# Two halves for the third query unit's channel mixing and for one GELU group (two-layer attention and mixer kernel)

## The chip, the core and the metric

The kernel runs on one core of a Trainium2 chip. The metric is the device time of one execution in microseconds. Five engines run their own instruction streams and meet at semaphores: TensorE (PE) multiplies, ScalarE (ACT) evaluates functions such as exp, tanh and GELU, VectorE (DVE) does elementwise work and moves results out of PSUM, GpSimd (POOL) computes here the powers for the normalisations, and SyncE (SP) issues the DMAs.

## The reference

Two layers; each is an attention block and a mixer with an MLP, both with residuals, over 2048 positions of 448 channels. The attention has 16 heads of 28 channels. Both layers use the same weights.

```python
# A: attention on the normalised x          (wo, wqkv)
p = softmax(einsum("bhqd,bhkd->bhqk", q, k) * 28**-0.5)
x = x + einsum("bhqk,bhkd->bhqd", p, v) @ wo
# B: mixer and MLP on y = layernorm(x)      (w1, w2, w3, w4)
h  = gelu(layernorm(y) @ w1)
hs = concat(four channel groups of h, shifted by -1, +1, -2, +2 positions) @ w2
x1 = y + hs
x  = x + x1 + gelu(layernorm(x1) @ w3) @ w4
```

## The kernel before

**Tiles and units.** A tile is 128 positions; there are 16. Attention works on query units: four units of four tiles, the last of layer 1 halved in two units of two tiles. Units are counted from 0, so the third is unit 2 with the tiles 8 to 11. For each unit and each group of four heads PE makes scores for one key tile after the other (L1243), ACT takes their exponential (L1269, two or three score blocks of 512 columns in one instruction), and PE multiplies with the values (L1318). Fifty score blocks get their exponential on DVE (L1159 to L1172). The sums over keys are normalised on DVE, and the output projection (L1386 and on) adds to the residual x_res.

**The mixer behind a unit.** When a unit's attention is done, `t_outproj` calls `spawn_mixer`, which starts two kinds of task. `t_mixA` normalises a list of tiles, transposes them, multiplies with w1 and applies the GELU; within the stretch this GELU is made of DVE operations around one tanh on ACT (`tanh_gelu`, L1406 to L1437). The transposes are a DMA on SP for more than two tiles, and PE transposes (L872, copied out at L877) for one or two (`n <= 2`). `t_mixB` takes groups of tiles from the table `MIXB`: it waits for mixA of the tiles beside them (the shift by positions), makes x1 (`t_x1`, w2), transposes, multiplies with w3 in 14 groups whose results DVE moves to h2T (L1609), and after a GELU on ACT multiplies with w4 (14 matmuls a tile). In layer 1 its transposes are on PE too for one or two tiles.

**The GELU groups.** An entry of `MIXB` is (tiles, first column slot in h2T, group). `t_gelu` waits until w3 is done for all entries of a group and then issues one GELU for each entry, back to back, so that exp's and GELU's tables are exchanged once per group. Entries without a group (the last three tiles) take their GELU straight from PSUM.

**Who sets the order.** A planner in the file (`Sched`) builds the instruction stream of every engine at build time from task generators with assumed durations, and tracks all reads and writes to place the semaphores. It plans some rounds; each uses latest starts from the round before, and `MOVES` lists, for two of them, times and random seeds at which the due times of some tasks are shifted. Other seeds give another order of the same work. Where the planner sees PE idle too long it inserts fill matmuls that compute nothing needed (L1686). In the setup some operations may run on ACT or on DVE (`alt`), as the planner finds it.

**The head.** Before the first exponential the kernel loads x and wqkv, casts wq and wk into padded form (L741, L743), normalises and transposes the first four tiles, and projects keys, queries and values of the first chunk (L662, L665 with wk_pad, wq_pad, wv). **The tail** after the last exponential is the last units' output projection, mixer and MLP, and the output stores.

Of the kernel before, what the change touches and what calls it, by code (L numbers as in the profile page):

```python
# [496 lines left out]
def build_kernel(nc, A_x, A_wqkv, A_wo, B_x, B_w1, B_w2, B_w3, B_w4, out, n_layers=2):  # L497
# [11 lines left out]
    BIAS2 = 127.0  # L509
    WSH = 60.0 / LN2 + BIAS2  # L510
    DEFER = 4
    OFFL = ((48, 104, 6), (104, 300, 6), (372, 411, 6), (480, 520, 6), (520, 600, 8), (640, 731, 6))
    EXPA = (0.07826797 * 128) ** (1 / 3)
    EXPB = EXPA * 0.30457565 / 0.07826797
# [3 lines left out]
    ROUNDS = 2  # L518
    MOVES = [
        [  # L520
            (0.00, 453789), (32.56, 797911), (48.62, 659924), (64.69, 318104), (161.61, 114807), (210.38, 918064), (274.54, 530462), (290.66, 355311),
            (306.74, 234581), (323.12, 940320), (355.32, 335807), (374.64, 262209), (390.75, 238473), (423.02, 904553), (455.14, 951219), (503.31, 353319),
            (519.32, 830975), (551.41, 87786), (567.44, 416536), (583.44, 953034), (599.45, 216641), (615.49, 123806), (647.71, 418804), (663.92, 737035),
            (679.96, 651820), (728.32, 723986), (760.36, 640052), (792.53, 320335), (808.54, 626538), (840.72, 608440), (876.72, 136641), (908.79, 748207),
            (924.80, 42066), (941.01, 696523), (957.18, 398650), (973.27, 754326), (989.39, 285914), (1006.15, 600949), (1022.18, 988087),
        ],
        [
            (0.00, 951844), (12.28, 444188), (24.31, 919282), (48.56, 963253), (60.73, 133731), (72.83, 242907), (84.87, 106861), (108.92, 980702),
            (133.43, 460163), (145.58, 489327), (157.59, 422286), (181.65, 400901), (205.74, 788872), (217.97, 738730), (230.17, 462143), (254.24, 124206),
            (266.43, 963194), (278.52, 170914), (290.57, 109033), (302.68, 722504), (314.77, 35337), (327.20, 201463), (339.27, 676445), (351.28, 477925),  # L530
            (366.34, 151894), (390.42, 723936), (402.46, 162311), (414.47, 812461), (426.52, 379211), (438.52, 122860), (450.61, 425742), (462.66, 818907),
            (475.22, 535633), (487.27, 1519), (499.30, 306556), (516.33, 162929), (540.73, 587464), (552.75, 370357), (564.75, 1541), (576.96, 165268),
            (589.01, 579738), (601.02, 905581), (613.58, 714602), (625.65, 696422), (637.83, 751260), (649.91, 220258), (661.93, 654573), (698.68, 121787),
            (710.99, 422722), (723.01, 142611), (735.05, 984297), (759.08, 14052), (771.10, 359944), (783.26, 84680), (795.40, 873617), (807.52, 132498),
            (819.69, 932845), (843.77, 139438), (855.88, 608162), (893.87, 524650), (905.88, 743153), (918.47, 135596), (942.74, 639761), (954.85, 280336),
            (966.90, 914942), (978.92, 414440), (1015.44, 282794), (1027.57, 425880), (1039.68, 28012),
        ],
    ]
    GATE1 = ('qr', 0)
# [12 lines left out]
    HALVED = [(4 * c, 4) for c in range(NCH - 1)] + [(NT - 4, 2), (NT - 2, 2)]  # L552
    MIXB = [
        [([0, 1, 2], 0, 0), ([3, 4, 5, 6], 3, 0), ([7, 8, 9, 10], 0, 1), ([11, 12], 4, 2), ([13, 14, 15], 0, 2)],
        [([0, 1, 2], 4, 0), ([3, 4, 5, 6], 0, 0), ([7, 8, 9, 10], 3, 1), ([11, 12], 0, 2), ([13], 2, None), ([14, 15], 3, None)],
    ]
    WHOLE = [(4 * c, 4) for c in range(NCH)]
    UNITS = [WHOLE] * (n_layers - 1) + [HALVED]
# [15 lines left out]
    def c_b2b(n):  # L574
        return 0.07 + n * 0.00026
# [8 lines left out]
    with st:  # L584
# [72 lines left out]
        def op(eng, dur, fn, reads=(), writes=(), **kw):  # L657
            return (eng, dur, fn, list(reads), list(writes), kw)
# [165 lines left out]
        def ln_stats(t):  # L824
            yield op("dve", 0.55, lambda e: e.bn_stats(out=st6[:, t, :], in_=x_res[:, t, :]), reads=[("x", t)], writes=[("st6", t)])  # L825
            yield op("dve", 0.2, lambda e: e.bn_aggr(out=mv[:, t, :], in_=st6[:, t, :]), reads=[("st6", t)], writes=[("mv", t)])
# [305 lines left out]
        def on_dve(n):  # L1132
            if len(grans[n]) < 3:
                return False
            L, u, g, p, kts, first, last = segs[grans[n][2][0]]
            return 1 <= grans[n][2][1] <= len(kts) * UNITS[L][u][1] // 4 - 4 and any(a <= n < b and n % m == 0 for (a, b, m) in OFFL)

# [142 lines left out]
        def t_pv(si):  # L1280
# [6 lines left out]
            for i in range(len(kts)):  # L1287
                if i % grp == 0:
                    now = [h for h in held if h[0] + DEFER <= i * nt // 4]
                    held = [h for h in held if h not in now]  # L1290
# [161 lines left out]
        def t_mixA(L, tiles, direct):  # L1452
            n = len(tiles)
            NW = 128 * n
            t0 = tiles[0]
            for t in tiles:
                for tp in (t - HR - 1, t - HR, t - HR + 1):
                    if 0 <= tp < NT:
                        yield ("wait", ("x1", L, tp))
                    elif L > 0 and 0 <= tp + NT < NT and NT % HR == 0:  # L1460
                        yield ("wait", ("x1", L - 1, tp + NT))
            for t in tiles:
                yield ("wait", ("x1r", L, t))
                yield from ln_stats(t)
            xs = yield from acq_xn(n, direct)
            sl = slice(t0, t0 + n)
            mk = [("mst", t) for t in tiles]
            mvk = [("mv", t) for t in tiles]
            yield op("dve", 0.1, lambda e: e.tensor_scalar(out=mst[:, sl, T1], in0=mv[:, sl, 1], scalar1=1.0 + EPS, scalar2=EPS * EPS, op0=ALU.mult, op1=ALU.add), reads=mvk, writes=mk)
            yield op("pool", 0.42 + 0.15 * n, lambda e: e.tensor_tensor(out=mst[:, sl, R12], in0=mst[:, sl, T1], in1=neghalf[:, 0:n], op=ALU.pow), reads=mk + [("neghalf",)], writes=mk)  # L1470
            yield ("spawn", t_r1(tiles), 3, True)
            for i, t in enumerate(tiles):
                yield op("dve", 0.12 + c_b2b(D), lambda e, t=t, i=i: e.tensor_scalar(out=blk(xs.v[:, i, :]), in0=b112(x_res[:, t, :]), scalar1=mv[:, t, 0:1], scalar2=mst[:, t, R12:R12 + 1],
                                                                          op0=ALU.subtract, op1=ALU.mult),
                         reads=[("x", t), ("mv", t), ("mst", t)], writes=[(xs.key, i)])
            xt = yield from acq_xt(n, direct)
            yield from transposes(xs, xt, n, direct or n <= 2)
            yield ("rel", xs.res)
            c0 = 2 + 128 * (t0 % HR)
            def group(grp):  # L1480
                b = yield ("acq", MISC, [xt.key])
                for (fc, rows) in KCM:
                    yield mm(NW, 112, lambda a, z, b=b: ps[a:z, bi(b), 0:NW], lambda a, z, fc=fc, rows=rows: w1[0:rows, fc, 112 * grp + a:112 * grp + z],
                        xt.v[0:rows, 0:n, fc, :], fc == 0, fc == 3,
                        reads=[xt.key, ("w1",)], writes=[("ps", bi(b))], touch=[b])
                hk = hkeys(grp, t0, tiles[-1])
                if direct:
                    yield op("act", c_act(NW), lambda e, grp=grp, b=b: e.activation(out=hT[0:112, grp, c0:c0 + NW], in_=ps[0:112, bi(b), 0:NW], func=ACT.Gelu_apprx_tanh),
                             reads=[("ps", bi(b))], writes=hk, touch=[b], tab="gelu")
                else:  # L1490
                    yield from tanh_gelu(hT[0:112, grp, c0:c0 + NW], ps[0:112, bi(b), 0:NW], 112, NW, b, hk)
                    return
                yield ("rel", b)
            yield from par(3, [group(grp) for grp in range(4)])
            yield ("rel", xt.res)
            for t in tiles:
                yield ("sig", ("mixA", L, t))
                if t % HR == 0 and t > 0:
                    yield ("spawn", t_halo(L, t), 2)
# [154 lines left out]
        def spawn_mixer(L, u):  # L1654
            t0, n = UNITS[L][u]
            end = u == len(UNITS[L]) - 1
            ta = list(range(t0, t0 + n))
            if end and L == n_layers - 1:
                for t in ta:
                    yield ("spawn", t_mixA(L, [t], True), 3)  # L1660
            else:
                yield ("spawn", t_mixA(L, ta, False), 3)
            last = max(t0 + n - 2, 0) if not end else NT - 1
            for (tiles, h0, k) in MIXB[L]:
                if max(t0 - 1, 0) <= tiles[-1] <= last and (tiles[-1] < NT - 1 or end):
                    yield ("spawn", t_mixB(L, tiles, h0, k, 3), 3)
# [110 lines left out]
```

## Time and profile before

| | us |
|---|---|
| median of 4 runs (1068.8, 1062.56, 1070.72, 1069.67) | 1069.24 |
| the profiled execution | 1068.8 |
| its span from first to last instruction | 1067.1 |
| ACT busy | 1019.0 (95%) |
| PE busy, fill matmuls L1686 among it | 1029.4 (96%), 139.7 |
| DVE busy | 745.4 (70%) |
| POOL busy | 58.0 (5%) |
| GELU instructions L1650 (9) | 44.9 |
| DMA transposes issued on SP, L866 | 29 records, 3.7 to landing (median) |

The profile describes one execution. A group's line gives its source line, engine and operation, tiles out<-in with their shapes and the count; behind the bar the busy time, the mean duration in ns of one instruction, and the time that the engine sat idle just before such instructions with what ended the wait. Consecutive ACT instructions overlap by a little, so the mean duration of one is more than the distance from start to start. Lines of a timeline begin with the start and the length in us. In a table of windows each engine's busy time is followed by its instruction count, and the columns at the end are the granted TensorE clock (1.00 is full), the DMA share and GB/s.

### The profile page before, as it was taken

How to read it: one execution, taken by the hardware profiler on the slowest of the kernel's cores; microseconds unless marked ns; L12 is line 12 of the kernel's file. 1: busy time of each engine (PE TensorE's matmuls, PEld its weight loads, DVE VectorE, ACT ScalarE, POOL GpSimd, SP SyncE). 2: the span in 40 equal slices, each digit the busy share in tenths (PEclk: the TensorE clock that was granted, in tenths of full speed). 3: DMA queues.
4: the chain of work that ended last, by engine and by line, in shares of the span. 5: the costliest groups of instructions: out<-in, count | busy, mean ns of one | idle time of the engine just before them, and what ended most of it. 6: DMA issues, size and time to landing. Idle time of an engine off the chain costs nothing.

```text
span 1067.1 us, 21975 instructions
## 1 busy us (share of the span) xinstructions
PE 1029.4 (96%) x9469; PEld 396.9 (37%) x9485; DVE 745.4 (70%) x1683; ACT 1019.0 (95%) x940; POOL 58.0 (5%) x78
## 2 busy tenths in 40 slices
PE   8999999999999999999999999999999999999998
PEld 4333333333333333332333433333333333444455
DVE  6976468876887547887579666557978864677644
ACT  5999999999999999999989999999999999999983
POOL 1100000000000001010001000000000000010000
PEclk9999899999999999999989999999999999999999
DMA  4233140000001001100111101212020001110000
GB/s 115 61 110 100 35 121 20 2 16 21 21 2 21 1 3 39 35 22 1 20 41 31 26 11 60 70 43 48 21 46 1 21 1 33 30 22 2 2 19 23
DMA packets 70714, 35.09 MB, mean 33 GB/s; under 512 B 56472, under 2 KB 65048, under 8 KB 70616
## 3 DMA queue, kind: packets, MB, share of 16 engines
q1 hardware_dynamic: 70616, 33.68, 12.6%
q8 instruction: 74, 1.21, 0.5%
q14 instruction: 24, 0.20, 0.1%
HBM read 12.70 MB, written 7.08 MB: 19 GB/s over the span
## 4 chain that ended last, share of the span: by engine, by line
ACT 53%; PE 41%; DVE 4%; DMA 1%; issue 1%; SPq 0%; POOL 0%; POOLq 0%; DVEq 0%; ACTq 0%
ACT PT L1269 46%; PE ps L662 11%; PE ps L1243 11%; PE ps L1318 9%; PE ps L1686 6%; ACT h2T L1650 4%; PE ps L665 3%; ACT L1650 1%; ACT gt L1433 1%; DMA h2T<-in_A_wqkv_dram 1%; ACT L1269 1%; DVE hT L1406 0%; DVE sq L941 0%; DVE qT L970 0%; PE ps L872 0%
## 5 line engine op out<-in xcount | busy, mean ns | idle before, releaser
L1269 ACT ACTIVATE PT<-ps 128x1024 bf16<-128x1024 f32 (+1 forms) x821 | 918.4, 1228 | 13.2 <-PE ps L1243 8.9
L1243 PE MATMUL ps<-qT,kT 32*128 32x512 bf16 (+1 forms) x2304 | 323.3, 362 | 15.5 <-ACT PT L1269 11.3
L1318 PE MATMUL ps<-PT,vaug 128*32 128x512 bf16 (+1 forms) x2253 | 268.9, 364 | 3.6 <-ACT PT L1269 2.3
L1243 PEld LDWEIGHTS ps<-qT,kT 32*128 32x128 bf16 x2304 | 80.7, 91 | 263.9 <-ACT PT L1269 160.3
L1686 PE MATMUL ps<-ones_bf 128*128 128x256 bf16 x893 | 139.7, 279 | 2.9 <-DVE hot L696 1.1
L1318 PEld LDWEIGHTS ps<-PT,vaug 128*32 128x32 bf16 x2253 | 67.6, 94 | 135.7 <-issue 82.8
L662 PE MATMUL ps<-xT,w 112*128 112x512 bf16 (+6 forms) x574 | 115.6, 320 | 1.2 <-DVE h2T L1609 0.4
L1609 DVE CAST h2T<-ps 128x512 bf16<-128x512 f32 (+2 forms) x126 | 73.6, 584 | 58.7 <-PE ps L662 43.6
L1686 PEld LDWEIGHTS ps<-ones_bf 128*128 128x128 bf16 x893 | 73.6, 99 | 68.7 <-issue 50.6
L665 PE MATMUL ps<-xT,w 112*32 112x512 bf16 (+3 forms) x808 | 71.9, 350 | 0.3 <-DVE qT L970 0.2
L662 PEld LDWEIGHTS ps<-xT,w 112*128 112x128 bf16 (+1 forms) x574 | 46.1, 104 | 46.0 <-issue 24.3
L662 PE MATMUL ps<-w,h2T 128*128 128x448 bf16 x257 | 61.2, 354 | 0.4 <-ACT h2T L1606 0.4
L1159 DVE TENSOR_SCALAR t<-ps 128x512 int32<-128x512 f32 x50 | 34.3, 686 | 32.7 <-PE ps L1243 32.2
L665 PE MATMUL ps<-w,h2T 128*32 128x448 bf16 x764 | 49.4, 353 | 3.8 <-ACT h2T L1650 2.4
L1650 ACT ACTIVATE h2T<-h2T 128x7168 bf16<-128x7168 bf16 (+2 forms) x9 | 44.9, 5012 | 0.1
L1347 DVE SCALAR_TENSOR_TENSOR uin<-uin,fct,ps 128x512 f32<-128x512 f32 x20 | 14.8, 742 | 38.8 <-PE ps L1318 38.2
L1568 POOL TENSOR_TENSOR mst<-mst,neghalf 128x1 f32<-128x1 f32 x32 | 25.5, 803 | 296.9 <-DVE mst L1566 296.9
L825 DVE BATCH_NORM_STATS2 st<-x_res 128x6 f32<-128x448 bf16 x64 | 38.9, 613 | 1.6 <-DMA x_res<-in_A_x_dram 0.9
L1626 DVE TENSOR_TENSOR uin<-x_res,ps 128x448 bf16<-128x448 bf16 x16 | 9.8, 615 | 38.9 <-PE ps L662 20.9
L1167 DVE SCALAR_TENSOR_TENSOR gt<-gt 128x512 f16<-128x512 f16 x50 | 34.5, 691 | 1.3
L1172 DVE SCALAR_TENSOR_TENSOR PTD<-t,gt 128x512 uint16<-128x512 int32 x50 | 34.5, 689 | 1.3
L1168 DVE SCALAR_TENSOR_TENSOR gt<-gt 128x512 f16<-128x512 f16 x50 | 34.4, 688 | 1.3
(143 smaller groups left out, 1043.5 us busy)
## 6 DMA issues: line engine op xcount, KB each, us to landing
uin<-uscr SPq DMA_DIRECT2D x20, 256.0 KB, 2.7
uscr<-u_sb SPq DMA_DIRECT2D x12, 256.0 KB, 2.0
uscr<-uin SPq DMA_DIRECT2D x8, 256.0 KB, 2.1
out_dram<-uin SPq DMA_DIRECT2D x16, 112.0 KB, 1.7
w<-in_B_w_dram SPq DMA_DIRECT2D x4, 392.0 KB, 3.7
x_res<-in_A_x_dram SPq DMA_DIRECT2D x3, 448.0 KB, 8.6
w<-in_B_w_dram SPq DMA_DIRECT2D x2, 448.0 KB, 7.2
h2T<-in_A_wqkv_dram SPq DMA_DIRECT2D x2, 392.0 KB, 5.9
```

The source lines that it names most:

```text
L662: return e.matmul(out=dst(0, m), lhsT=lhs(0, m), rhs=rhs, start=start, stop=stop)
L665: return [e.matmul(out=dst(a, min(m, a + 32)), lhsT=lhs(a, min(m, a + 32)), rhs=rhs, start=start, stop=stop, tile_position=(0, a)) for a i ...
L825: yield op("dve", 0.55, lambda e: e.bn_stats(out=st6[:, t, :], in_=x_res[:, t, :]), reads=[("x", t)], writes=[("st6", t)])
L1167: yield op("dve", c_ps(512), lambda e: e.scalar_tensor_tensor(out=ex, in0=fx, scalar=-EXPA, in1=fx, op0=ALU.add, op1=ALU.mult), reads=[((" ...
L1168: yield op("dve", c_ps(512), lambda e: e.scalar_tensor_tensor(out=ex, in0=fx, scalar=EXPB, in1=ex, op0=ALU.add, op1=ALU.mult), reads=[(("g ...
L1172: yield op("dve", 0.06 + c_ps(512), lambda e: e.scalar_tensor_tensor(out=PTD[:, slot, :].bitcast(mybir.dt.uint16), in0=t32[:, :], scalar=2 ...
L1243: yield op("pe", 0.005 if ph == h else 0.012 + W / 2400.0, lambda e, bk=bk, r0=32 * j, g=g, kc=kc, q0=q0, W=W, c0=W * h: e.matmul(out=ps[: ...
L1269: yield op("act", e_dur(n), lambda e, b0=b0, p0=p0, cnt=cnt: e.activation(out=PT[:, p0:p0 + cnt, :], in_=ps[:, b0:b0 + cnt, :], func=ACT.E ...
L1318: yield op("pe", nt * 0.054 if item in late else 0.004 + nt * 0.0133, lambda e, j=j, rhs=rhs, vs=vs, i=i: e.matmul(out=ps[32 * j:32 * j + ...
L1609: yield op("dve", c_ps(NW), lambda e, fch=fch, b=b: e.tensor_copy(out=h2T[:, fch, hoff:hoff + NW], in_=ps[:, bi(b), 0:NW]), reads=[("ps", ...
L1650: yield op("act", c_act(14 * NW), lambda e, c0=c0, NW=NW: e.activation(out=h2T[:, :, c0:c0 + NW], in_=h2T[:, :, c0:c0 + NW], func=ACT.Gelu ...
L1686: SC.fill = (0.13, lambda e, b: e.matmul(out=ps[:, bi(b), 0:256], lhsT=ones_bf[:, :], rhs=ones_bf[:, :].unsqueeze(1).to_broadcast([128, 2, ...
```

## The change

`HALFA` names layer 1, unit 2. For it `spawn_mixer` starts two `t_mixA` tasks of two tiles (8, 9 and 10, 11) where it started one of four. In layer 1's `MIXB` the entry of tiles 7 to 10 becomes two entries of two tiles, at slots 3 and 5 of h2T, both still in group 1; so there are two `t_mixB` tasks, each with PE transposes, and `t_gelu` issues two GELUs of 2 x 128 columns by 14 where it issued one of 4 x 128. The seeds in `MOVES` are other ones, too (39 and 69 became 40 and 59), so the planner's order differs everywhere from the first instructions on.

```diff
+    HALFA = ((1, 2),)
...
     MOVES = [
-            (0.00, 453789), (32.56, 797911), (48.62, 659924), (64.69, 318104), (161.61, 114807), (210.38, 918064), (274.54, 530462), (290.66, 355311),
+            (0.00, 453789), (16.37, 681098), (32.56, 797911), (48.64, 673494), (64.65, 986619), (112.91, 402327), (129.29, 347222), (193.63, 37042),
...
     MIXB = [
...
-        [([0, 1, 2], 4, 0), ([3, 4, 5, 6], 0, 0), ([7, 8, 9, 10], 3, 1), ([11, 12], 0, 2), ([13], 2, None), ([14, 15], 3, None)],
+        [([0, 1, 2], 4, 0), ([3, 4, 5, 6], 0, 0), ([7, 8], 3, 1), ([9, 10], 5, 1), ([11, 12], 0, 2), ([13], 2, None), ([14, 15], 3, None)],
...
-                yield ("spawn", t_mixA(L, ta, False), 3)
+                step = 2 if (L, u) in HALFA else n
+                for k in range(0, n, step):
+                    yield ("spawn", t_mixA(L, ta[k:k + step], False), 3)
```

## The prediction

> **What bounds the kernel now.** I read the page's part 1, then the chain that ended last, then what ScalarE (ACT) waits for, then the head, the throttled places and the tail in the timeline.
>
> From the page, the shares of the chain, the exponential's group of part 5, and the pairs of ACT's waits:
>
> ```profile
> ACT 53%; PE 41%; DVE 4%; DMA 1%; issue 1%; SPq 0%; POOL 0%; POOLq 0%; DVEq 0%; ACTq 0%
> ...
> L1269 ACT ACTIVATE PT<-ps 128x1024 bf16<-128x1024 f32 (+1 forms) x821 | 918.4, 1228 | 13.2 <-PE ps L1243 8.9
> ```
>
> ACT is busy 1019.0 of 1067.1 us, and 918.4 of these are the 821 exponentials. Before them it idles only 13.2 us. So the run has three stages: a head until the first exponential, a stretch in which ACT sets the pace, a tail after the last exponential. PE's 96% misleads: 139.7 us of it are fill matmuls (L1686) and most of the rest lies under ACT.
>
> Head and tail in the timeline:
>
> ```profile
> 26.27 2.76 PE L662 MATMUL ps<-xT,wq_pad 112*128 112x512 bf16 x12
> ...
> 29.69 3.71 ACT L1269 ACTIVATE PT<-ps 128x1536 bf16<-128x1536 f32 x3
> ...
> 1030.54 3.19 ACT L1650 ACTIVATE h2T<-h2T 128x3584 bf16<-128x3584 bf16 x1
> ...
> 1049.25 6.51 PE L662 MATMUL ps<-xT,w 112*128 112x256 bf16 x60
> ...
> 1057.07 7.17 PE L662 MATMUL ps<-w,h2T 128*128 128x448 bf16 x37 [0.36 <-ACT h2T L1606]
> ```
>
> The first exponential starts at 29.69, right behind twelve query-projection matmuls. The last ends at 1029.25, where the table load before the last GELU starts. So head 29.7, stretch 999.6, tail 37.8 us.
>
> Where the stretch loses time, by windows (PE, PEld, DVE, ACT, POOL busy, then the granted clock):
>
> ```profile
> 548.00:550.00 2.00, 1.48 (x27) 0.73 (x27) 2.00 (x9) 1.84 (x4) 0.00 (x0) 1.00 0.05 12
> 550.00:552.00 2.00, 1.81 (x13) 0.73 (x13) 2.00 (x9) 2.00 (x2) 0.00 (x0) 0.86 0.00 0
> 552.00:554.00 2.00, 2.00 (x17) 0.67 (x14) 1.77 (x6) 1.48 (x2) 0.00 (x0) 0.50 0.90 206
> 554.00:556.00 2.00, 2.00 (x13) 1.14 (x11) 0.51 (x3) 1.02 (x1) 0.00 (x0) 0.50 0.25 56
> ```
>
> After a thin patch of PE the clock falls to half, and ACT starves: its idle gaps from 554 to 564 are 0.67, 1.34, 1.27, 0.42 and 0.40, together 4.1 us. A second such place, 111 to 118, costs 0.54 + 1.31 = 1.85 us. So about 6 of the 13.2 us are the clock's; the remaining 7 are scattered over some 900 us.
>
> **The change part by part.** The edit is small, but the planner also gets other random moves, so the order of nearly everything changes. I compared the two instruction orders engine by engine. The exponentials (821, same widths) and the scores are the same; what differs is below.
>
> *ACT, on the path.* Rows for the two edited operations:
>
> ```profile
> L1650 ACT ACTIVATE h2T<-h2T 128x7168 bf16<-128x7168 bf16 x4 | 24.7, 6169 | 0.0
> ...
> L1650 ACT ACTIVATE h2T<-h2T 128x3584 bf16<-128x3584 bf16 x2 | 6.4, 3190 | 0.0
> ```
>
> One 7168-wide GELU (6.18) becomes two of 3584. Back to back, a 3584 and a 5376 take 7.83 and a 5376 alone 4.68, so the first costs 3.15: 3.15 + 3.19 − 6.18 = +0.16. Both keep group 1, so they stay behind one table load: six GELU loads in both orders. Four 512-wide tanh (L1433; start to start with the next exponential 0.52) become eight of 256 (0.31): 2.48 − 2.08 = +0.40. Together **+0.56 us**, all on the path.
>
> *DVE, hidden.* Tanh-GELU chain: eight times 1.64 (0.42+0.29+0.23+0.29+0.41) less four times 2.50 = +3.1. Evictions L1609: 28 of 0.422 for 14 of 0.687 = +2.2. Copies of PE transposes (L877): 8 of 0.42 = +3.4. Sum +8.7 us on an engine that is 70% busy; cost 0. Without the cover ACT would wait for a tanh input, which in this profile it did for 0.8 us over all tanh. POOL gets two more powers (0.5 to 0.8 each, 5% busy): 0.
>
> *PE and SP.* Halves of two tiles are transposed by PE instead of by DMA: 32 more matmuls L872, two fewer DMA transposes on SP. The stationary loads of w3 double (4 x 14 more, 0.10 each, overlapped). The moving columns stay the same. 32 x 0.11 = 3.5 us of PE. Cover: my sums of each stretch of 40 score blocks by these rows leave PE 1 to 8 us below ACT per 18 us in both orders. SP loses the transposes (3.7 us to landing) and gains nothing; its spills, reloads and outputs stay at their places beside them. Each half takes one of the two xn and one of the two xT buffers, so both halves shut out other users for a while: a projection that comes late for it would show as ACT waiting for scores, of which the nearest row (L1269) has 13.2 us over 821 exponentials, the longest 1.3. So 0 to 1.3; I take 0, as no scores in that stretch wait for a new projection of more than one unit.
>
> *The moved GELU.* Group 1 stands behind exponential 807 now and behind 792 in the new order, about 15 exponentials (17 us) earlier. What hangs on it is the w4 matmuls of tiles 7 to 10. Before, 83 w4 matmuls remain after the last exponential; in the new order exactly 70, those of tiles 11 to 15. The 13 that go are worth 13 x 0.19 = 2.5 us of PE, but of these 11 run at 1029.4 to 1033.3 while PE waits for the last GELU anyway, so they are nearly free. What the tail really gains: the output add of tile 10 (0.58, L1626) leaves DVE's queue ahead of the residual adds (0.3 of it waited for), and 14 w4 matmuls move from behind the last w3 group into it. There PE needs 56 x 0.109 + 42 x 0.194 = 14.2 us from 1049.25 on against 15.0 now (to 1064.24), −0.8. Sum **−1.1** (bounds 0 and −2.5).
>
> *The head.* Before, 48 projection matmuls of 448 or 512 columns precede the first scores (wk 16, wq 16, wv 16); now 32 (wk 12, wq 4, wv 16). Twelve wq took 2.76 (row above), four wk 2.91/3 = 0.97: −3.7 us ahead of the first exponential. The two first pad casts and one xn move from ACT to DVE, so ACT's last xn comes earlier: −0.6, halfway between 0 and one xn plus one cast (1.3). But these 16 matmuls, their evictions (now on DVE: 3 x 0.684 + 0.745) and squares come back between the first exponentials. There PE has 1.4 us of slack in the first 17 us by my sums and none in the next 17 (2.7 and 1.1 before). Cost between 0 and the whole 3.7; in this profile 30 to 40 us, the nearest, ACT lost 0.2 us while doing much the same. I take **+1.0**. Head net **−3.3**.
>
> *The clock, where a rule speaks against the change.* The window above holds two blocks of four transposes (at 551.05 and 551.95) where PE counts as 90% busy, and the clock still falls. The other thin places (370 to 373 at 62% busy, 517 to 520 at 67%) held clock 1.00. The Trainium skill, "TensorE: Matmul & The Clock Gate", Part 4, says that transposes do not count as PE activity for the clock gate in the way that matmuls do. By the rule, 32 more transposes in the last 200 us open more such places, each at 1.85 to 4.1 us: one makes the sum 1069.1. By the row, other transposes in the stretch (634 to 638, and 999) ran at clock 1.00, so most cost nothing and the sum stays 1065.0. I take 0 and keep +4 (and −4 for a place that stays warm in the new order) for the range. The new order has 37 more fill matmuls, two of them beside the transposes in question.
>
> Sum against the profiled execution's 1068.8 us (1067.1 of span): 1068.8 + 0.6 − 1.1 − 3.3 = 1065.0, with the scattered waits left unchanged. The median shown, 1069.24, is 0.4 above this execution, so the difference of **−3.8 us** stands for either. Predicted: **1065.0 us**.
>
> **The rivals.** *Nothing is left of it:* the late projections starve ACT at head groups 1 to 3, the whole 3.7 is returned, 1065.0 + 2.7 = 1067.7. For it: no slack from 17 to 34 us after the start. Against: the order puts them between granules, no block longer than some 2 us.
>
> *Slower, by the clock gate:* PE transposes and the thin patches around them drop the clock at three of the four new transpose groups; at 4.1 each 1065.0 + 12.3 = 1077.3. It decides from the first: one place (4.1) eats the whole 3.8. For it: 548 to 562, and the rule. Against: the fill matmuls, and that only two places in the stretch's thousand microseconds did so.
>
> *Faster than forecast:* the place at 551 depends on which matmuls happen to lie in a window; in the new order w1 groups and two fills stand beside those transposes. Without it 1065.0 − 4.1 = 1060.9. For it: one of the four runs shown took 1062.56, 6 us under the others, about the two places together.
>
> *The change does not do what it says:* excluded; both halves and both GELUs stand in the new order.
>
> **How the numbers follow.** Forecast 0.50 with its own range 1062 to 1068 (its head term from −4.3 to −1, tail to −2.5); nothing left 0.18; clock gate, slower, 0.13; fewer cold places 0.19. A change under 0.5% (5.3 us: 1063.5 to 1074.1) is about what can't be told from none. Of the forecast, 0.19 lies below 1063.5; with the last rival's 0.19 and 0.03 from mixtures, faster 0.41. The slow rival alone lies above 1074.1: slower 0.13; the rest, 0.46, is within. The range takes in the forecast, the first and the last rival with 3 us below it for a second place gone, and one cold place too many with the head's gain returned (1065.0 + 4.1 + 3.7): 1058 to 1073. Only the slow rival and a little below 1058 stay out.
>
> **What would show it.** First exponential at 25 to 26.5 us; ACT's idle before L1269 in the first 40 us of the stretch at most 1.5 us; L1650 0.2 us longer at six loads; from the last exponential to the end 36 to 37.5 us; L872 x104; DVE some 9 us busier. Wrong would be: an idle before L1269 well over 13 us without cold windows (the order itself fails), cold windows beside L872 after 850 us (the slow rival), or a first exponential still near 29.

## The result and the profile after

The changed kernel takes **1064.38 us** (median of 42 executions, 1060.44 to 1070.51) against 1067.2 (63 executions, 1060.51 to 1071.91) of the kernel before on the same chips: ratio 0.9975, 95% interval 0.9963 to 0.9986. The 0.25% lie outside the noise of the comparison, and inside the 0.5% that the prediction called indistinguishable from no change. The lowest times of both are equal within 0.1 us.

The profiled execution took 1066.58 us (span 1064.2). From its page, the chain and the exponential's group:

```profile
ACT 57%; PE 34%; DVE 6%; DMA 2%; issue 1%; SPq 0%; DVEq 0%
...
L1269 ACT ACTIVATE PT<-ps 128x1024 bf16<-128x1024 f32 (+1 forms) x821 | 918.1, 1224 | 15.7 <-PE ps L1243 11.9
```

ACT bounds it still, and waits *more* ahead of its exponentials than before: 15.7 against 13.2 us. The waits that PE's scores end rose by 3.0, from 8.9 to 11.9. Split as in the prediction:

| stage | before | after | difference |
|---|---|---|---|
| head, to the first exponential | 29.69 | 24.43 | −5.26 |
| stretch, to the last GELU's table load | 999.56 | 1002.86 | +3.30 |
| tail | 37.85 | 36.91 | −0.94 |

What became of the shorter head stands in the timelines of ACT, DVE and PE, and in the window from 24 to 36 us (columns as in the tables of windows):

```profile
24.43 4.63 ACT L1269 ACTIVATE PT<-ps 128x1536 bf16<-128x1536 f32 x4
30.94 2.37 ACT L1269 ACTIVATE PT<-ps 128x1536 bf16<-128x1536 f32 x2 [1.89 <-PE ps L1243]
34.92 15.93 ACT L1269 ACTIVATE PT<-ps 128x1536 bf16<-128x1536 f32 x14 [1.61 <-PE ps L1243]
...
33.94 0.35 DVE L1195 TENSOR_SCALAR qT<-qT,bcol 128x512 bf16<-128x512 bf16 x1
...
34.13 0.39 PE L662 MATMUL ps<-xT,wk_pad 112*128 112x512 bf16 x1 [0.44 <-DMA xT<-xn]
34.45 0.60 PE L1243 MATMUL ps<-qT,kT 32*128 32x512 bf16 x5
...
24.00:36.00 12.00, 10.47 (x84) 3.51 (x86) 11.30 (x33) 8.42 (x8) 3.03 (x6) 1.00 0.20 45
```

Four exponentials, a wait of 1.89 us, two more, a wait of 1.61 us. The seventh, at 34.92, is the first that reads the second group of queries. DVE adds that group's bias (L1195), the last step before its scores, from 33.94 to 34.29, and the scores start at 34.45. Just ahead of them in its queue PE does a key projection that had waited 0.44 us for a DMA.

The clock, by windows (PE, PEld, DVE, ACT, POOL busy, then the granted clock):

```profile
14.00:19.00 5.00, 3.81 (x41) 2.06 (x40) 3.52 (x16) 2.10 (x3) 0.55 (x1) 1.00 0.02 5
109.00:123.00 14.00, 13.63 (x63) 3.88 (x65) 6.73 (x13) 10.61 (x10) 0.00 (x0) 0.51 0.02 2
546.00:562.00 16.00, 15.94 (x155) 6.50 (x153) 14.77 (x41) 15.60 (x16) 0.00 (x0) 1.00 0.24 51
850.00:1027.00 177.00, 171.21 (x2300) 77.11 (x2300) 108.90 (x284) 176.69 (x155) 8.43 (x12) 1.00 0.04 10
```

One cut of the clock remains in this profile, at 109 to 123 us. The place near 551 is gone, and so is a cut at 14 to 19 us in the head, which I had not looked for in the profile of before; its row there is

```profile
14.00:19.00 5.00, 4.70 (x35) 2.24 (x36) 2.37 (x16) 1.34 (x3) 1.30 (x2) 0.66 0.02 5
```

In the tail's timeline the last GELU starts right behind the last exponential, and 28 w4 matmuls stand behind the last w3 group (42 before):

```profile
1027.29 1.28 ACT L1650 ACT_TABLE_LOAD   x1
...
1054.23 1.80 PE L662 MATMUL ps<-xT,w 112*128 112x256 bf16 x15
1055.87 5.46 PE L662 MATMUL ps<-w,h2T 128*128 128x448 bf16 x28
```

**Time against clock.** Each execution comes with its mean granted clock. For the 99 executions of the kernel before from the time of the experiments (those of the first experiment among them), and the 43 of the changed kernel that carry a clock:

| mean granted clock | before: executions, median us | after: executions, median us |
|---|---|---|
| 0.998 and more | 13, 1062.5 | 13, 1062.0 |
| 0.995 to 0.998 | 24, 1064.5 | 9, 1062.4 |
| 0.993 to 0.995 | 20, 1066.3 | 16, 1065.9 |
| 0.990 to 0.993 | 25, 1067.8 | 3, 1066.5 |
| below 0.990 | 17, 1070.7 | 2, 1070.5 |

A straight line through each gives 1060.81 us at clock 1 and 0.85 us per 0.001 of clock for the kernel before (correlation −0.98), 1060.84 and 0.76 for the changed one (−0.92). At full clock the two meet (the lines are good to about 0.3 us there). Their mean clocks are 0.9933 and 0.9955, their mean times 1066.51 and 1064.23. On the line of before, 0.9955 stands for 1064.6: so of the 2.3 us, about 1.9 are clock, and 0.4 are left for everything else.

### The profile page after: what moved, and what is told of

It is laid out like the page before. It is cut to its first block, busy times and chain, and to the rows that moved or that the text cites. A ratio compares the mean times of both kernels' runs of the same rounds, so it can differ in the third digit from the quotient of the medians.

```text
span 1064.2 us, 21662 instructions
## 1 busy us (share of the span) xinstructions
PE 1022.4 (96%) x9279; PEld 400.7 (38%) x9296; DVE 743.9 (70%) x1734; ACT 1015.7 (95%) x938; POOL 57.0 (5%) x80
## 4 chain that ended last, share of the span: by engine, by line
ACT 57%; PE 34%; DVE 6%; DMA 2%; issue 1%; SPq 0%; DVEq 0%
ACT PT L1269 50%; PE ps L662 9%; PE ps L1243 9%; PE ps L1318 7%; PE ps L1688 6%; ACT h2T L1650 4%; PE ps L665 2%; DMA xT<-xn 2%; ACT gt L1433 1%; ACT L1650 1%; DMA h2T<-in_A_wqkv_dram 1%; ACT L1269 0%; DVE hT L1437 0%; DVE hT L1406 0%; DVE kT L934 0%
## 5 line engine op out<-in xcount | busy, mean ns | idle before, releaser
L1269 ACT ACTIVATE PT<-ps 128x1024 bf16<-128x1024 f32 (+1 forms) x821 | 918.1, 1224 | 15.7 <-PE ps L1243 11.9
L1318 PE MATMUL ps<-PT,vaug 128*32 128x512 bf16 (+1 forms) x2253 | 245.7, 363 | 2.5 <-ACT PT L1269 1.2
L662 PE MATMUL ps<-xT,w 112*128 112x256 bf16 (+6 forms) x632 | 120.8, 311 | 0.8 <-DVE h2T L1609 0.3
L1609 DVE CAST h2T<-ps 128x256 bf16<-128x256 f32 (+2 forms) x140 | 75.5, 539 | 47.2 <-PE ps L662 28.7
L662 PE MATMUL ps<-w,h2T 128*128 128x448 bf16 x326 | 75.8, 354 | 3.6 <-ACT h2T L1650 2.2
L665 PE MATMUL ps<-xT,w 112*32 112x256 bf16 (+4 forms) x864 | 63.5, 323 | 0.2 <-DVE hT L1406 0.2
L1650 ACT ACTIVATE h2T<-h2T 128x3584 bf16<-128x3584 bf16 (+2 forms) x10 | 44.9, 4528 | 0.1
L662 PEld LDWEIGHTS ps<-w,h2T 128*128 128x128 bf16 x326 | 27.9, 97 | 34.4 <-issue 13.3
L1633 DVE TENSOR_TENSOR x_res<-x_res,ps 128x448 bf16<-128x448 bf16 x16 | 9.7, 619 | 38.8 <-PE ps L662 24.8
L665 PE MATMUL ps<-w,h2T 128*32 128x448 bf16 x488 | 33.4, 354 | 3.1 <-ACT h2T L1650 3.1
L1168 DVE SCALAR_TENSOR_TENSOR gt<-gt 128x512 f16<-128x512 f16 x50 | 34.3, 687 | 1.1
```

Of the source, the lines that this page charges most:

```text
L662: return e.matmul(out=dst(0, m), lhsT=lhs(0, m), rhs=rhs, start=start, stop=stop)
L665: return [e.matmul(out=dst(a, min(m, a + 32)), lhsT=lhs(a, min(m, a + 32)), rhs=rhs, start=start, stop=stop, tile_position=(0, a)) for a i ...
L1168: yield op("dve", c_ps(512), lambda e: e.scalar_tensor_tensor(out=ex, in0=fx, scalar=EXPB, in1=ex, op0=ALU.add, op1=ALU.mult), reads=[(("g ...
L1269: yield op("act", e_dur(n), lambda e, b0=b0, p0=p0, cnt=cnt: e.activation(out=PT[:, p0:p0 + cnt, :], in_=ps[:, b0:b0 + cnt, :], func=ACT.E ...
L1318: yield op("pe", nt * 0.054 if item in late else 0.004 + nt * 0.0133, lambda e, j=j, rhs=rhs, vs=vs, i=i: e.matmul(out=ps[32 * j:32 * j + ...
L1609: yield op("dve", c_ps(NW), lambda e, fch=fch, b=b: e.tensor_copy(out=h2T[:, fch, hoff:hoff + NW], in_=ps[:, bi(b), 0:NW]), reads=[("ps", ...
```

## The experiments

All but the first and the two with exchanged seeds keep a planned order and replay it with a few operations moved or added after the planner's last round; in all but the first, lines stand one off those above (mostly L1270 for L1269). "At clock 1" is the value of such a line through an experiment's own 10 to 12 executions (6 for the exchanged seeds), good to about 1 us.

**Is it the order or the clock?** The kernel before once more, unchanged.

> The kernel before, unchanged, to read time against mean granted clock execution by execution. Theory A (order): the new order is 2.4 us shorter at any clock (head -2.0, tail -1.0, wider ACT work +0.6), so executions of before at a clock of 0.998 or more take 1063 us or more, where the changed kernel took 1060.4 to 1063.5. Theory B (clock): at equal clock both take the same, so these executions take 1060.4 to 1062, and before is slower only because its clock is cut more often. Both: about 0.76 us per 0.001 of mean clock.

1068.16 us, ratio 1.0013 [0.9991, 1.0035], mean clock 0.992, 1061.1 at clock 1. Windows of its profiled execution:

```profile
14.00:19.00 5.00, 4.88 (x37) 2.27 (x35) 2.45 (x17) 1.30 (x3) 1.15 (x2) 0.66 0.02 5
109.00:125.00 16.00, 15.25 (x74) 4.43 (x75) 7.00 (x13) 12.16 (x11) 0.00 (x0) 0.57 0.11 38
550.00:566.00 16.00, 15.14 (x124) 5.62 (x119) 9.92 (x34) 11.97 (x11) 0.38 (x1) 0.68 0.18 45
```

Three cuts, one of them in the head. Its one execution at a clock of 0.998 or more took 1062.52, between the two theories; the lines above speak for B. Then both kernels got three fill matmuls ahead of each of the score groups for exponentials 66 to 74, where the cut at 110 us begins:

```diff
+        LO, HI, PER = 66, 75, 3
...
+            if score and not run and LO <= e < HI:
+                b = free_bank(k)
+                if b is not None:
+                    seq += [("pe", lambda x, b=b: ffn(x, "b%d" % b), (("ones_bf",),), (("ps", b),), (), False) for _ in range(PER)]
```

> The changed kernel with three fill matmuls ahead of each score group between exponentials 66 and 74, where its profile shows a thin patch of PE just before the clock is cut at 109 us. If the cut follows from the thin patch, the cut is gone, the mean clock is 0.997 or more and the median 1061.5 to 1062.5 (2 to 3 us less than the changed kernel). If the cut does not depend on it: 1064.4 or up to 0.5 more, with the cut still at 109 to 123.

> The same fill matmuls in the kernel before, at the same exponentials (its cut is at 111 to 118 us). Theory A (order): 2.4 us above the changed kernel with fill, so about 1064.5. Theory B (clock): the same as that kernel within 0.7 us, about 1062, apart from what its second cut at 551 costs.

Changed kernel with fills: 1063.97, ratio 0.9985 [0.9967, 1.0003], mean clock 0.9981, 1062.7 at clock 1. Kernel before with fills: 1065.46, ratio 1.0000 [0.9978, 1.0022], mean clock 0.9968, 1063.3 at clock 1. At clock 1 the two lie 0.6 us apart, within what such a line can tell, where theory A asked for 2.4: theory B again. The fills keep the mean clock up, and cost about 2 us at full clock: in the changed kernel ACT then waits 1.8 us for scores at 100 to 130, the cut gone. So neither gains much, and they are no better version. Their use is that the profiled execution of the kernel before with fills has no cut anywhere (clock 1.00 over the span of 1061.7; the changed one 0.998 and 1062.5, with a cut of 3.4 us at 675 to 680). There the old order can be read at full clock, first in windows, then in ACT's timeline:

```profile
14.00:19.00 5.00, 4.05 (x36) 2.05 (x36) 3.52 (x21) 2.02 (x4) 1.42 (x2) 1.00 0.02 5
109.00:125.00 16.00, 15.32 (x114) 6.17 (x116) 6.06 (x11) 14.85 (x14) 0.00 (x0) 1.00 0.07 20
550.00:563.00 13.00, 12.58 (x134) 5.63 (x134) 10.89 (x31) 11.95 (x12) 0.55 (x1) 1.00 0.23 62
```

```profile
28.04 5.98 ACT L1270 ACTIVATE PT<-ps 128x1536 bf16<-128x1536 f32 x5
34.18 6.92 ACT L1270 ACTIVATE PT<-ps 128x1024 bf16<-128x1024 f32 x6 [0.16 <-PE ps L1244]
```

The first exponential at 28.04 instead of 29.69: of these 1.65 us PE was 0.2 ahead already at 13 us, and the other 1.4 or so of the old head were the cut at 14 to 19 us. The sixth exponential starts at 34.18 and lasts 0.95, so the seventh starts at about 35.1. In the changed kernel it starts at 34.92. Three more profiles of the changed order, from here and from below (with the three fills, with three moved places, and with these and one fill), are the same up to there; they have the first exponential at 23.73 to 24.55 and the seventh at 34.22 to 34.91. **Of a head that starts 3.5 to 4.3 us earlier at full clock, 0.2 to 0.9 us are left seven exponentials later.** From the first to the seventh it is 7.1 us in the old order and 10.4 to 10.7 in the new one.

**What returns the head's gain?** First the sixteen moved projections were put back ahead of the first scores:

```diff
+        P = replay(P.all[:first] + early + late + P.all[end:])
```

> The changed kernel with all 16 moved key and query projections put back ahead of the first scores, as before; nothing else moves. If the shorter head is what is left of the gain: first exponential at 28 to 29 us instead of 24.4, the 3.5 us of ACT idle at 29 to 35 gone, and 1.5 to 2.5 us slower than the changed kernel, about 1066.5. If the head's gain was returned in full: the same time, 1064.4 within 0.5.

1070.57, ratio 1.0031 [1.0009, 1.0053], 1064.6 at clock 1. No theory had this right: the first exponential came at 32.20 and not at 28 to 29. Ahead of it PE waited 0.63 and 1.05 us for DVE to evict kT and qT (the kernel before had four of the evictions of q on ACT, the changed kernel has one), and the clock was cut. Waits of 0.34 and 2.44 us remain behind the fourth and the sixth exponential; the second lies in another cut:

```profile
29.00:33.00 4.00, 3.57 (x33) 0.83 (x25) 2.63 (x6) 0.80 (x1) 0.00 (x0) 0.57 0.58 131
36.00:43.00 7.00, 6.46 (x26) 2.00 (x28) 4.19 (x11) 4.22 (x4) 0.00 (x0) 0.51 0.01 2
```

The edit also takes along whatever depends on the delayed scores, so that DVE's work on the queries waited 5.44 us for them. With all this in it, the run does not tell what returned the head's gain; it shows only that this order is slower, by 3.8 us at clock 1.

Then the scores were moved ahead, with the normalisation of the second query group ahead of the third's on DVE:

```diff
+        mid = [285, 288, 286, 287, 289, 291, 292, 293, 294, 290, 304, 306, 309, 310, 303, 307, 305, 308, 312,
+               318, 320, 321, 322, 323, 324, 325, 331, 334] + list(range(295, 303)) + [335, 343, 344, 346, 348,
...
```

> The changed kernel with its own order, save 72 instructions at 27 to 35 us: scores of the fifth to eighth exponential are moved ahead of the second half of the sixteen q projections and of the k projection that waits for the transposed unit; the normalisation of the second q group is moved ahead of that of the third; four fill matmuls there are left out. Theory return (the waits of 1.89 and 1.61 us after the fourth and sixth exponential are the matmuls and the normalisation that stood in front of the scores; the shorter head is given back there): ACT idle before exponentials in 20 to 64 us falls from 3.7 to 0.4 to 1.2, the last exponential ends 2.5 to 3.3 us earlier, and at equal clock the time is 2 to 3 us below the changed kernel, a line through about 1058 to 1059 at clock 1, median near 1061.5. Rival theory later wait (the scores moved ahead push the projections of the following groups back, and the wait comes again some exponentials later, or the fct or transposed unit is what really limits): idle stays near 3.5 in 20 to 130 us, time unchanged within 0.5 us at equal clock. Rival clock: a change of the cuts (the first unit's matmuls are rearranged) hides or doubles the gain; to be read from the mean clock.

1066.81, ratio 1.0011 [0.9989, 1.0033], 1062.9 at clock 1, some 2 us above the changed kernel. Its ACT timeline, and a window:

```profile
23.46 4.62 ACT L1270 ACTIVATE PT<-ps 128x1536 bf16<-128x1536 f32 x4
29.20 2.37 ACT L1270 ACTIVATE PT<-ps 128x1536 bf16<-128x1536 f32 x2 [1.12 <-PE ps L1244]
32.14 2.37 ACT L1270 ACTIVATE PT<-ps 128x1536 bf16<-128x1536 f32 x2 [0.58 <-PE ps L1244]
39.81 1.45 ACT L1270 ACTIVATE PT<-ps 128x1536 bf16<-128x1536 f32 x1 [5.30 <-PE ps L1244]
...
36.00:39.00 3.00, 2.95 (x8) 1.19 (x9) 2.21 (x7) 0.00 (x0) 0.00 (x0) 0.50 0.00 0
```

With DVE's order changed the seventh exponential does start earlier, at 32.14, 8.68 us behind the first instead of 10.49. The ninth then waits 5.30 us: its scores stand on PE behind seven key projections, and ahead of these PE waited 0.48, 0.71 and 0.79 us for DVE. The seven ran at half clock and took 2.98 us, where six of them take 1.47 in the changed kernel, so about 1.3 of the 5.30 (an estimate from these two) go to a cut. The rival "later wait" had the mechanism; the three waits came to 7.0 and not 3.5 us. Last, only the scores moved, and DVE's order stayed. This kernel leaves one wait out: the first two score blocks of the second group are made from q before its bias is added (L1195; L1196 here), right behind the product before it (L971). So it is no version to use, only a look at what the seventh exponential waits for.

```diff
+        ahead([318, 320, 321, 322], 304)
+        ahead([323, 324, 325], 311)
...
+        ahead([344, 346, 348], 342)
```

> The changed kernel with its own order, save that the scores of the fifth to seventh exponential are moved ahead of the matmuls that stand in front of them at 28 to 34 us (three fill matmuls there are left out); VectorE's order is untouched. Theory second group (the seventh exponential is the first that reads the second query group, whose q is normalised on VectorE at 34.3 us whatever PE does with the scores; VectorE has no idle time from 25 to 40 us): the wait of 1.89 us before the fifth exponential is gone, the fifth and sixth run to 31.5, and the seventh waits 3.5 to 4.5 us and starts at 35 to 36 us, no earlier than the 34.92 of the changed kernel; at equal clock the time is that of the changed kernel or up to 1 us more: a line through 1061 to 1062 at clock 1. Theory scores (the waits are only scores queued behind other matmuls): idle in 20 to 64 us falls from 3.7 to below 1.5, the seventh exponential starts before 33 us, and the line goes through 1058 to 1059.

1063.57, ratio 0.9971 [0.9949, 0.9993], 1061.0 at clock 1 (changed kernel 1060.8). Timeline of ACT and of DVE:

```profile
23.46 6.89 ACT L1270 ACTIVATE PT<-ps 128x1536 bf16<-128x1536 f32 x6
34.03 2.37 ACT L1270 ACTIVATE PT<-ps 128x1536 bf16<-128x1536 f32 x2 [3.68 <-PE ps L1244]
...
32.80 0.75 DVE L971 SCALAR_TENSOR_TENSOR qT<-ps,sc,qT 128x512 bf16<-128x512 f32 x1
```

Six exponentials in a row, then one wait of 3.68 where there were 1.89 and 1.61. From the first exponential to the seventh it is 10.57 us here and 10.49 in the changed kernel. Two waits have become one of about the same length, because the seventh exponential is due when DVE has worked through the second query group: moving scores on PE alone does not bring it forward. With the bias waited for it would come some 0.35 us later still (an estimate, from the length of L1195 above). DVE is not alone in this chain, as here it waited 0.47 and 0.21 us for the query projections that the scores had pushed back. That is the theory "second group", at its lower end of 3.5 to 4.5 us; "scores" fell.

**Which part of the change?** The diff has two parts, the split and the list of seeds. Each alone; the first is shown, the second is the opposite exchange in the kernel before:

```diff
     MOVES = [
-            (0.00, 453789), (16.37, 681098), ...
+            (0.00, 453789), (32.56, 797911), ...
```

> The changed kernel with the split alone: third unit in halves and the GELU group in two groups, but the list of seeds of the kernel before. Nothing is left out. In this order 17 projections of the first unit stand ahead of the first scores (kernel before 28 of q and k and 16 of v, changed kernel 12+4 of q and k and 16 of v). Theory clock (the seeds only chose an order, all orders are near each other at full clock): a line of time against mean granted clock through 1060.5 to 1063 at clock 1 with about 0.8 us per 0.001, so the median is set by how often the clock is cut; between 1062 and 1069. Theory split (the split itself brings the gain, by a tail 0.9 us shorter and softer needs of the units): 1064 to 1065, below the kernel before by 2 to 3 us, tail 36.9 us. Theory seeds (the gain is that of the new list, the split costs its +0.5 us of ACT): 1067 to 1070.

> The kernel before with the new list of seeds alone: third unit whole and its four-tile GELU group whole. Nothing is left out. In this order 24 projections of q and k and 16 of v stand ahead of the first scores. Theory clock: again a line through 1060.5 to 1063 at clock 1; the median anywhere between 1062 and 1069, as the clock is cut. Theory split: 1067 or more, as the kernel before. Theory seeds: 1064 to 1065 as the changed kernel. In all three the GELU group of four tiles takes one table load and about 12.4 us in two instructions.

All theories failed, mine foremost. Split with the old seeds: **1127.33 us**, ratio 1.0581 [1.0554, 1.0607]. New seeds without the split: **1117.78**, ratio 1.0484 [1.0448, 1.0520]. At clock 1 they are 1122.8 and 1111.3, so this is order, not clock. The first exponentials of the split with the old seeds, and DVE's addition of the second query group's bias:

```profile
23.19 2.36 ACT L1270 ACTIVATE PT<-ps 128x1536 bf16<-128x1536 f32 x2
26.48 2.37 ACT L1270 ACTIVATE PT<-ps 128x1536 bf16<-128x1536 f32 x2 [0.93 <-PE ps L1244]
29.12 2.36 ACT L1270 ACTIVATE PT<-ps 128x1536 bf16<-128x1536 f32 x2 [0.28 <-PE ps L1244]
57.19 6.89 ACT L1270 ACTIVATE PT<-ps 128x1536 bf16<-128x1536 f32 x6 [25.70 <-PE ps L1244]
...
56.11 0.60 DVE L1196 TENSOR_SCALAR qT<-qT,bcol 128x512 bf16<-128x512 bf16 x1
```

The earlier first exponential goes with the slowest kernel of all: the seventh waits 25.70 us for the second group, which is ready at 56.71. A seed list belongs to the exact task set for which it was found; the split cannot be valued apart from it, and these two runs say nothing for or against the split.

**Can the waits that are left be taken out?** At three places of the changed kernel an exponential waits over 1 us at full clock; the matmuls that it waits for were moved ahead of others.

```diff
+        ahead([4077, 4078, 4079], 4072)
+        ahead([4896, 4906, 4907, 4908], 4893)
+        ahead([5000, 5001, 5002, 5003, 5004, 5005, 5006], 4988)
```

> The changed kernel with its own order, save at three places where an exponential waits in its profile: three scores moved ahead of four of the eight matmuls of a channel mixing at 441 us (wait 1.21), three scores ahead of seven matmuls of the values at 532 us (wait 1.11), seven matmuls of the values ahead of five of another kind at 539 us (wait 1.32). Theory places (each wait is local, and what is moved back has slack): the three waits fall to 0 to 0.4 each, 2.5 to 3.4 us in all, at equal clock the time falls by as much: a line through 1057.5 to 1058.5 at clock 1, median 1061 to 1062.5 at a mean clock near 0.9955. Rival (what is moved back makes another exponential late within 10 us): one or two of the three come back, 0.5 to 1.5 us gained. Rival (the last exponential is not what ends the time): nothing gained, which the tail of 36.9 us after it speaks against.

1066.42, ratio 0.9991 [0.9968, 1.0014], 1061.8 at clock 1: nothing gained. In its ACT timeline:

```profile
437.14 1.45 ACT L1270 ACTIVATE PT<-ps 128x1536 bf16<-128x1536 f32 x1 [0.35 <-PE ps L1244]
439.67 0.63 ACT L1434 ACTIVATE gt<-gw 112x512 f32<-112x512 f16 x1 [1.08 <-DVE gw L1423]
...
528.33 2.37 ACT L1270 ACTIVATE PT<-ps 128x1536 bf16<-128x1536 f32 x2 [0.76 <-PE ps L1319]
...
539.60 2.37 ACT L1270 ACTIVATE PT<-ps 128x1536 bf16<-128x1536 f32 x2 [1.41 <-PE ps L1244]
```

The wait of 1.21 fell to 0.35, and the tanh behind it, whose input comes by way of the w1 matmuls that were pushed back, now waits 1.08. 1.11 became 0.76 with another releaser, 1.32 became 1.41. The first rival had the mechanism, but not even its 0.5 us were gained.

Two last tries for a faster kernel put one fill matmul instead of three ahead of each score group at 110 us, with the moved scores of the head and with the three moved places:

> As the kernel with the moved scores, and one fill matmul of 256 columns (0.12 to 0.28 us) ahead of each of nine score groups for exponentials 66 to 74, where the clock is cut at 109 to 123 us in the changed kernel; with three of them there the cut was gone and ACT waited 1.8 us more at 100 to 130 us. Theory busy share (the cut follows PE being idle some of each 3 us there): one fill keeps the clock uncut in most executions, mean clock above 0.997, and costs 0.3 to 0.8 us: median 1059.5 to 1061. Rival (one is not enough, the cut stays): mean clock near 0.9955, median near that of the kernel with the moved scores plus 0 to 0.5. Rival (price of fills is the order, not their number): 1.5 us or more are lost at full clock.

> As the kernel with three moved places, and one fill matmul of 256 columns ahead of each of nine score groups for exponentials 66 to 74 (109 to 123 us). Theory busy share: the cut of the clock at 109 to 123 us goes in most executions, mean clock above 0.997, price 0.3 to 0.8 us: median 1059.5 to 1061.5, below the kernel with the moved places by 0.5 to 2. Rival (one fill is not enough): mean clock near 0.9955, median that of the kernel with the moved places plus 0 to 0.8.

1067.45, ratio 1.0014 [0.9991, 1.0037], mean clock 0.9945; and 1065.40, ratio 0.9973 [0.9950, 0.9996]. In the second, one execution of twelve took 1099.89, at a clock of 0.849. The other eleven have a mean clock of 0.9966 (0.9943 without the fills): three are at 1.000, two at 0.990. The profiled one is of the latter and has

```profile
100.00:125.00 25.00, 23.38 (x140) 6.95 (x138) 13.93 (x25) 20.42 (x19) 0.00 (x0) 0.73 0.10 30
```

One fill does not keep the cuts away reliably. No version that clearly beats the changed kernel was found.

## Why the prediction was right, and where it was wrong

The forecast of 1065.0 us is 0.6 above the median, the difference −3.8 against −2.8. The sum came out near the mark, but by other terms than its own: the head gave back nearly all that it was to bring, and a term set to zero, the clock, brought about as much. That is luck. At equal clock the terms as measured (head −0.2 to −0.9, tail −0.9, ACT's content +0.8) add up to −0.3 to −1.0, and the two lines lie 0.0 apart at clock 1.

- **ACT's content, +0.56: right in kind, 0.2 low.** The two GELUs took 6.27 together instead of 6.18, +0.09 for +0.16, behind six table loads as said. The tanh rows went from 19.6 to 20.3, +0.7, where start-to-start distances gave +0.40.
- **DVE, +8.7 hidden: the rows right, the total not.** The named rows grew by 2.6 (tanh chain), 1.9 (L1609) and 3.2 (L877), 7.7 in all, yet the engine's own busy time went from 745.4 to 743.9. Hidden it is.
- **PE and SP, 0: consistent.** L872 x104 as said. At 900 to 1010 us, where the halves run, ACT waits 0.2 us ahead of exponentials instead of 1.8 (one wait, for PE's products with the values).
- **Tail, −1.1: −0.94, right.**
- **Head, −3.3: the step that failed.** The head became 5.26 shorter. Some 1.4 of this was a cut of the clock that I had not seen. Against the old head without a cut it is 3.6 shorter, and 3.5 to 4.3 over four profiles; this stands for the sixteen projections and the earlier xn (3.7 and 0.6 in the prediction). The term *"I take +1.0"* for what comes back was mis-sized: at full clock 3.3 to 3.6 us came back within seven exponentials, near the upper bound of 3.7. I looked for slack of PE between the exponentials. The limit of the seventh was a chain on DVE, which was busy for 11.3 of the 12 us from 24 to 36: evict, square, multiply, add the bias, of the second query group. The key projection in PE's queue that waits for a DMA added little: in the four profiles the scores start 0.02 to 0.38 us behind the end of the bias.
- **Clock, 0 with ±4: the term that decided.** The sum left the clock out, and about 1.9 of the 2.3 us between the means are the clock's. I had named it as a rival ("the place at 551", chance 0.19); the place is gone in the changed kernel's profile, with the one in the head.
- **The rule on transposes:** the row was right to be preferred. All 24 transposes at 914 to 940 us and the 24 after them ran at clock 1.00 (the window 850 to 1027 above), as four-groups did before at 634 to 638 and 999. The rule of the Trainium skill ("TensorE: Matmul & The Clock Gate", Part 4) is not tested here for a transpose alone; applied as I did, to count cold places by groups of transposes, it gave one to three too many. The slow rival fell.
- **"Nothing left":** at full clock this is what happened, by the mechanism named for it, late projections, with DVE in PE's place for the seventh exponential. Its 1067.7 missed, as the clock moved too.
- **Signs:** first exponential at 24.43 (25 to 26.5 said), waits in the first 40 us of the stretch 3.7 (at most 1.5 said), tail 36.91 (36 to 37.5 said).

Why the new order has fewer cuts is not settled. In the head, both profiles of the unmodified kernel before show the cut at 14 to 19 us, and that of the changed kernel does not; but the old head with fills put in at 110 us ran without it too, though nothing ahead of it differs. By place the profiles differ more clearly. The cut near 551 is in two of the three of the old order and in none of the eight of the new order (the changed kernel and its replays). At 674 to 685 six of these eight have a cut of 3.4 us, and none of the three. The place near 110 is cut in both orders, for 3.4 to 13.7 us, but not in every execution. So an order makes a cut likelier or less likely at a given place, and I haven't isolated by what.

## What to carry to other kernels

An earlier first instruction on the bounding engine is worth only what is still there at its next late input: follow the second and the third input of that engine back to the engine that makes them, before adding up what the first gains. Where times of one kernel scatter by more than the change under study, fit time against granted clock for both kernels and compare at equal clock. And a planner's random seeds are part of the version: exchanging them alone cost 50 to 63 us here, while no other edit moved the time by more than some 6.

## What the runs showed of the hardware

- A kernel's executions lie on a line of time against mean granted clock, with 0.68 to 0.97 us per 0.001 in all kernels (the single time of 1099.89 left out). 0.001 of 1062 us is 1.06 us, so most of the lost clock reaches the end of this kernel.
- In a cut the clock is at half. With that, the windows above give the cuts' lengths: 3.4 us for 0.66 over 5 us, 10.2 for 0.68 over 16, 13.7 for 0.51 over 14. These are about one, three and four times 3.4.
- While the clock is cut PE does not look idler: 94 to 98% busy in the head's window, against 76 to 81% at full clock, and 95 to 97% with and without a cut in the windows at 109 to 125 and from 550 on. The column of the granted clock shows a cut; the busy share does not.
- The same place, behind the same instructions, is cut in one execution (14 to 19 us in the kernel before) and not in another (the same kernel with fills that come only at 110 us).
